# Two sums of g for the second MoE product: adding DMA transfers from GpSimd in place of VectorE, with B12, B22, T2 and T3 kept negated

## The chip, the cores and the metric

The kernel runs on one core of a Trainium2 chip. The metric is the device time of one execution in microseconds. The core has TensorE (PE in the profile, its weight loads PEld), VectorE (DVE), ScalarE (ACT), GpSimd (POOL) and SyncE (SP, which here only issues transfers). All work of an engine is done in the order in which the program gives it to that engine.

## The reference

```python
# q, k, v: (8, 12, 448, 64)
scores = scale * q @ k.T - log(S)
x = (sigmoid(scores) @ v), heads put side by side          # (3584, 768)
h = x @ w_in                                               # w_in  (768, 2048)
g = h * clip(h + 3, 0, 6) / 6
out = g @ w_out                                            # w_out (2048, 768)
```

Everything is float32.

## The kernel before

After the attention stage both MoE products are made by the scheme of Winograd and Strassen: each operand is cut into 2 x 2 blocks, sums of blocks are formed, and seven products M1 to M7 replace eight. Each float32 factor is split into two parts of a shorter type (`split`, lines 68 to 74: ScalarE casts the high part, L71, and VectorE subtracts it from the factor to get the low part, L73), and each product is three passes on TensorE.

The first product leaves h in blocks. `post` (from L404) puts each block together: ScalarE copies partial results out of PSUM (L384), VectorE adds them to the accumulator D or B (`added`, L388), ScalarE takes the relu of the block plus 3 (`relu`, L379), and VectorE makes min(relu, 6) * h (`gate`, L370). That gives the blocks B11, B21, B22 and B12 of g (without the factor 1/6). GpSimd makes T3 = B22 - B12 (L393) and T2 = T3 + B11 (L395). These six are stored to HBM (`gd`, L375).

The second product consists of 56 units (L437). A unit is one product of the seven, one of four pairs of batches, and one of two halves of the inner dimension; the order is M1, M2, M6, M7, M5, M4, M3, with 8 units for each. A unit is 3 x 4 x 3 = 36 matrix products (L657) of 128 x 128 by 128 x 448. Its operand is a block of g of 128 x 4 x 448 (896 KB). Five of the seven products take a stored block as it is. M5 (units 32 to 39) takes T1 = B12 - B11 and M4 (units 40 to 47) takes T4 = B21 - T2, which aren't stored; they are formed here:

- `g_load` (L450) loads the first block into the tile `gr` of the unit. There are three pools, one `gr` and one split tile `gx` in each, so units n and n + 3 share their tiles.
- `g_load2` (L457) loads the second block in two halves of 448 KB into two tiles of a ring of five.
- `g_sum` (L462) subtracts the halves from `gr` on VectorE.
- `g_split` splits `gr` into `gx`.

In turn n of the loop over units the program issues `g_load2` for unit n + 3, `g_load` for unit n + 4, what is planned for this turn (weight splits at each change of product, stores of results), then `g_sum` and `g_split` for unit n + 2, then the 36 products of unit n, and after each second unit `post2`: VectorE multiplies the PSUM result by 1/6 and adds it to a kept sum (`stt`, L591), once or twice. The order of the work on each engine is that of this program; no scheduler changes it. The weights of a product are loaded by SP (L472) and split at the turns around its first unit.

Of the kernel before, what the change touches and what calls it, by code (L numbers as in the profile page):

```python
# [8 lines left out]
F32 = mybir.dt.float32  # L9
# [3 lines left out]
AF = mybir.ActivationFunctionType  # L13
ALU = mybir.AluOpType
ENG = mybir.EngineType

B, H, S, D = 8, 12, 448, 64
DM, DF = 768, 2048
P = 128
# [20 lines left out]
M1, M2, M3, M4, M5, M6, M7 = range(7)  # L40
A11, A12, A21, A22, S1, S2, S3, S4 = range(8)
WEIGHT = {M1: A11, M2: A12, M3: S4, M4: A22, M5: S1, M6: S2, M7: S3}
B11, B21, B22, T4, T1, T2, T3, B12 = range(8)
MOVING = {M1: B11, M2: B21, M3: B22, M4: T4, M5: T1, M6: T2, M7: T3}
# [50 lines left out]
def tile_kernel(ctx: ExitStack, tc: tile.TileContext, qk, vP, wi, wo, outT):  # L95
    nc = tc.nc
    scale = 1.0 / math.sqrt(D)
# [4 lines left out]
    def dram_tile(name, shape):  # L102
        return dram.tile(shape, F32, name=name, tag=name)
# [4 lines left out]
    gd = {  # L108
        (p, k, h): dram_tile(f"gd_{p}_{k}_{h}", [P, FC, S])
        for p in range(NPR)  # L110
        for k in (B11, B21, B22, B12, T2, T3)
        for h in range(2)
    }
# [19 lines left out]
    bias_3 = dw.tile([P, 1], F32, name="bias_3")  # L133
# [7 lines left out]
    def ring(name, shape, dtype):  # L141
        return dw.tile(shape, dtype, tag="ring", name=name, bufs=5)

    def temp(tag, bufs, name, shape=(P, 2, S)):
        return tmp.tile(list(shape), F32, tag=tag, name=name, bufs=bufs)
# [12 lines left out]
    def at_slot(n, f, *a):  # L158
        later.setdefault(n, []).append((f, a))

    def at_unit(n, f, *a):
        plan.setdefault(n, []).append((f, a))
# [125 lines left out]
    for u in range(4 * EC):  # L288
        kh, ec = divmod(u, EC)
# [38 lines left out]
    for s in range(NS + LAG):  # L328
# [6 lines left out]
        m, r = divmod(s, LC)  # L335
# [7 lines left out]
    acc, quad = {}, {}  # L343
# [32 lines left out]

    def relu(q, k, h, tag, bufs):
        r = temp(tag, bufs, f"g{k}_{q}")
        nc.scalar.activation(r, h, AF.Relu, bias=bias_3, scale=1.0)  # L379
        return r  # L380

    def copied(q, key):
        acc[key, q] = temp("a", 4, f"{key}_{q}")
        nc.scalar.copy(acc[key, q], acc["A", q][:, :, :S])  # L384

    def added(q, key, name):
        c = temp("y", 2, f"c{name}_{q}")
        nc.vector.tensor_tensor(out=c, in0=acc[name, q][:, :, :S], in1=acc[key, q], op=ALU.add)  # L388
        return c

    def g_sums(q):
        t3 = temp("T", 3, f"gT3_{q}")
        nc.gpsimd.tensor_tensor(out=t3, in0=quad[q, B22], in1=quad[q, B12], op=ALU.subtract)  # L393
        t2 = temp("T", 3, f"gT2_{q}")
        nc.gpsimd.tensor_tensor(out=t2, in0=t3, in1=quad[q, B11], op=ALU.add)  # L395
        quad[q, T3], quad[q, T2] = t3, t2

    def c22(q, n):
        c = added(q, "u3", "D")
        at_slot(n + 1, gate, q, B22, c, relu(q, B22, c, "qk", 4))  # L400
        at_slot(n + 3, store, q, B22)

    def post(i, q, n):
        if i == M1:  # L404
            copied(q, "s1")
        elif i == M6:
            copied(q, "u2")
        elif i == M7:
            copied(q, "u3")
            if ("D", q) in acc:  # L410
                at_slot(n + 1, c22, q, n + 1)
        elif i == M5:
            if ("u3", q) in acc:
                c22(q, n)
        elif i == M2:
            c = added(q, "s1", "B")
            at_slot(n + 1, gate, q, B11, c, relu(q, B11, c, "v", 3))
            at_slot(n + 3, store, q, B11)
        elif i == M4:
            h = acc["A", q][:, :, :S]  # L420
            at_slot(n + 1, gate, q, B21, h, relu(q, B21, h, "qk", 4))
            at_slot(n + 3, store, q, B21)
        elif i == M3:
            c = added(q, "u2", "D")
            at_slot(n + 1, gate, q, B12, c, relu(q, B12, c, "qk", 4))
            at_slot(n + 2, g_sums, q)
            at_slot(n + 3, store, q, B12)
            at_slot(n + 4, store, q, T3)
            at_slot(n + 4, store, q, T2)
# [8 lines left out]
    gset, gr, gs, gx = [], {}, {}, {}  # L438
# [4 lines left out]
    PARTS = {T1: (B12, B11), T4: (B21, T2)}  # L443
# [8 lines left out]
    def g_load2(n):  # L452
        if n < len(units) and MOVING[units[n][0]] in PARTS:
            i, p, h = units[n]
            gs[n] = [ring(f"gr_{n}_{k}", [P, 2, S], F32) for k in range(2)]
            for k in range(2):
                nc.sync.dma_start(out=gs[n][k], in_=gd[p, PARTS[MOVING[i]][1], h][:, 2 * k : 2 * k + 2])  # L457

    def g_sum(n):
        for k, o in enumerate(gs.pop(n, ())):  # L460
            part = gr[n][:, 2 * k : 2 * k + 2]
            nc.vector.tensor_tensor(out=part, in0=part, in1=o, op=ALU.subtract)  # L462

    def g_split(n):
        gx[n] = gset[n % 3].tile([P, 2, FC, S], F32R, tag="gx", name=f"gx_{n}")
# [54 lines left out]
    for n, (i, q) in enumerate(seq):  # L520
        for f, a in later.pop(n, []):
            f(*a)
        w1_load(n + LA + 2)
        product(i, q, n)
        post(i, q, n)
# [31 lines left out]
    for h, n in ((0, 0), (1, 8)):  # L557
        for e in range(2 * EC):
            k, ec = divmod(e, EC)
# [9 lines left out]
    for k, i in enumerate(PHASES[1:]):  # L569
        n = 8 * (k + 1)  # L570
# [16 lines left out]
    po, so = {}, {}  # L587
    SIXTH = 1.0 / 6.0

    def stt(out, ps_in, other):  # L590
        nc.vector.scalar_tensor_tensor(out=out, in0=ps_in, scalar=SIXTH, in1=other, op0=ALU.mult, op1=ALU.add)  # L591

    def put(p, eh, k, o):
        nc.sync.dma_start(out=outT[2 * p + k, eh * EC : (eh + 1) * EC].rearrange("e p t -> p e t"), in_=o)
# [1 line left out]
    def out_tile(i, p):  # L596
        return acc_ctx[0].tile([P, EC, S], F32, tag="o", name=f"o_{i}_{p}", bufs=2)

    def kept(i, p):
        return acc_ctx[0].tile([P, EC, S], F32, tag="s", name=f"s_{i}_{p}", bufs=2 * NPR)  # L600

    def post2(i, p, n):
        t = po.pop(p)
        if n < len(units) - 1:
            t = t[:, :, :S]
        if i == M1:
            so[p] = kept(i, p)
            nc.scalar.mul(so[p], t, SIXTH)
        elif i == M6:
            stt(so[p], t, so[p])  # L610
        elif i == M7:
            so["u3", p] = kept(i, p)
            stt(so["u3", p], t, so[p])
        else:
            eh, k, other = {M2: (0, 0, p), M5: (1, 1, ("u3", p)), M4: (1, 0, ("u3", p)), M3: (0, 1, p)}[i]
            o = out_tile(i, p)
            if n == len(units) - 1:
                for ec in range(EC):
                    stt(o[:, ec], t[ec], so[other][:, ec])
                    nc.sync.dma_start(out=outT[2 * p + k, eh * EC + ec], in_=o[:, ec])  # L620
                return
            stt(o, t, so[other])
            if i == M5:
                stt(so[p], t, so[p])
            at_unit(n + 1, put, p, eh, k, o)

    for n, (i, p, h) in enumerate(units):
# [10 lines left out]
        for f, a in fetch.pop(n, []):  # L638
            f(*a)
        g_load2(n + 3)  # L640
        g_load(n + 4)
        for f, a in plan.pop(n, []):
            f(*a)
        if n + 2 < len(units):
            g_sum(n + 2)
            for _ in g_split(n + 2):
                pass
# [16 lines left out]
        if h == 1:  # L664
            post2(i, p, n)
# [34 lines left out]
```

## Time and profile before

| what | value |
|---|---|
| median of three runs | 1076.69 us (1075.88 to 1077.53) |
| the profiled execution | 1077.52 us, its span 1075.7 us |
| TensorE busy | 1067.0 us (99%) |
| VectorE busy | 743.0 us (69%) |
| ScalarE busy | 561.2 us (52%) |
| GpSimd busy | 174.2 us (16%) |
| clock granted to TensorE | 1.00 |
| second product | from about 667 us to the end |
| sums of L462 | 32 of 1084 ns, from 885.9 to 998.9 us |

Rows of groups read: line of the kernel, engine, operation, result <- operands, shapes, count | busy us, mean ns of one | idle time of the engine before them and who ended it. Rows of transfers end in the size of one and the median time in us from its issue to its landing. SPq is SP's queue of issues, L-numbers are lines of the kernel before. A share of DMA is the mean over the core's 16 DMA engines.

### The profile page before, as it was taken

How to read it: one execution, taken by the hardware profiler on the slowest of the kernel's cores; microseconds unless marked ns; L12 is line 12 of the kernel's file. 1: busy time of each engine (PE TensorE's matmuls, PEld its weight loads, DVE VectorE, ACT ScalarE, POOL GpSimd, SP SyncE). 2: the span in 40 equal slices, each digit the busy share in tenths (PEclk: the TensorE clock that was granted, in tenths of full speed). 3: DMA queues.
4: the chain of work that ended last, by engine and by line, in shares of the span. 5: the costliest groups of instructions: out<-in, count | busy, mean ns of one | idle time of the engine just before them, and what ended most of it. 6: DMA issues, size and time to landing. Idle time of an engine off the chain costs nothing.

```text
span 1075.7 us, 16712 instructions
## 1 busy us (share of the span) xinstructions
PE 1067.0 (99%) x6784; PEld 890.4 (83%) x6784; DVE 743.0 (69%) x713; ACT 561.2 (52%) x612; POOL 174.2 (16%) x82
## 2 busy tenths in 40 slices
PE   9999999999999999999999999999999999999998
PEld 4443466666999989999999999998999999999998
DVE  4679856642577987799888665987864437787642
ACT  7888988886446554664465555434332313222420
POOL 0214130000143345235322221200000000000000
PEclk9999999999999999999999999999999999999999
DMA  8887998874666877688766878869885376898741
GB/s 323 299 306 275 336 350 320 312 269 154 248 213 207 295 250 229 204 283 272 233 190 213 286 238 280 303 268 319 328 314 190 111 273 222 287 347 287 272 147 52
DMA packets 81484, 277.13 MB, mean 258 GB/s; under 512 B 7936, under 2 KB 22272, under 8 KB 81408
## 3 DMA queue, kind: packets, MB, share of 16 engines
q1 hardware_dynamic: 81408, 276.07, 73.0%
q8 instruction: 53, 0.87, 0.3%
q14 instruction: 23, 0.19, 0.0%
HBM read 189.92 MB, written 86.11 MB: 257 GB/s over the span
## 4 chain that ended last, share of the span: by engine, by line
PE 88%; DVE 4%; DMA 4%; issue 2%; ACT 2%; SPq 0%; ACTq 0%; DVEq 0%
PE po L657 32%; PE A L359 19%; PE sc L197 11%; PE pv L214 11%; PE D L359 9%; PE B L359 5%; DMA ws<-dw 2%; PE pl L657 1%; DVE w L73 1%; DMA dw<-w2S 1%; DMA qk<-qk 0%; ACT gx L71 0%; DVE x L73 0%; ACT a L199 0%; PE idle L322 0%
## 5 line engine op out<-in xcount | busy, mean ns | idle before, releaser
L657 PE MATMUL po<-gx,w 128*128 128x448 f32 x1944 | 390.0, 362 | 1.0 <-ACT w L71 0.7
L657 PEld LDWEIGHTS po<-gx,w 128*128 128x128 f32 x1944 | 364.3, 188 | 26.6 <-DVE w L73 1.4
L359 PE MATMUL A<-x,w 128*128 128x448 f32 x1152 | 236.1, 362 | 1.9 <-ACT u L384 1.9
L359 PEld LDWEIGHTS A<-x,w 128*128 128x128 f32 x1152 | 215.9, 188 | 17.6 <-ACT u L384 2.6
L71 ACT CAST gx<-gr 128x1792 fp32r<-128x1792 f32 x56 | 94.8, 1695 | 204.8 <-PE po L657 113.1
L214 PE MATMUL pv<-a,v 64*64 64x448 f32 x1344 | 198.8, 537 | 1.0 <-DVE xr L225 0.6
L197 PE MATMUL sc<-qk 64*64 64x448 f32 x1344 | 198.3, 537 | 0.4 <-ACT a L199 0.4
L199 ACT ACTIVATE a<-sc,bias_s 128x896 f32<-128x896 f32 x168 | 168.3, 1009 | 44.2 <-PE sc L197 41.3
L73 DVE TENSOR_TENSOR w<-ws,w 128x768 fp32r<-128x768 f32 x112 | 148.9, 1338 | 26.3 <-ACT w L71 26.0
L73 DVE TENSOR_TENSOR gx<-gr,gx 128x1792 fp32r<-128x1792 f32 x56 | 113.3, 2023 | 77.3 <-ACT gx L71 77.2
L214 PEld LDWEIGHTS pv<-a,v 64*64 64x64 f32 x1344 | 70.1, 133 | 62.8 <-issue 38.9
L197 PEld LDWEIGHTS sc<-qk 64*64 64x64 f32 x1344 | 69.3, 133 | 61.9 <-issue 29.2
L359 PE MATMUL D<-x,w 128*128 128x448 f32 x576 | 120.4, 362 | 0.0
L359 PEld LDWEIGHTS D<-x,w 128*128 128x128 f32 x576 | 108.1, 188 | 7.1
L71 ACT CAST w<-ws 128x768 fp32r<-128x768 f32 x112 | 93.0, 830 | 32.2 <-DMA ws<-dw 32.1
L393 POOL TENSOR_TENSOR gT<-g,g 128x896 f32<-128x896 f32 x16 | 43.5, 2721 | 269.7 <-DVE g L370 269.7
L225 DVE TENSOR_TENSOR xr<-pv,y 128x448 f32<-128x448 f32 x48 | 29.8, 621 | 53.7 <-ACT y L224 53.7
L359 PE MATMUL B<-x,w 128*128 128x448 f32 x288 | 60.2, 362 | 0.0
L379 ACT ACTIVATE g<-cD,bias 128x896 f32<-128x896 f32 x32 | 33.5, 1045 | 46.6 <-DVE cD L388 24.8
L359 PEld LDWEIGHTS B<-x,w 128*128 128x128 f32 x288 | 54.0, 188 | 3.6
L384 ACT COPY u<-A 128x896 f32<-128x896 f32 x32 | 29.0, 907 | 45.6 <-PE A L359 45.6
L388 DVE TENSOR_TENSOR cD<-D,u 128x896 f32<-128x896 f32 x32 | 34.8, 1088 | 21.0 <-ACT u L384 13.0
(65 smaller groups left out, 773.7 us busy)
## 6 DMA issues: line engine op xcount, KB each, us to landing
gr<-gd SPq DMA_DIRECT2D x56, 896.0 KB, 5.6
ws<-dw SPq DMA_DIRECT2D x112, 384.0 KB, 3.9
gd<-g SPq DMA_DIRECT2D x64, 448.0 KB, 4.6
qk<-qk SPq DMA_DIRECT2D x48, 448.0 KB, 6.7
gd<-gT SPq DMA_DIRECT2D x32, 448.0 KB, 5.2
gr<-gd SPq DMA_DIRECT2D x32, 448.0 KB, 6.1
wi<-wi SPq DMA_DIRECT2D x16, 768.0 KB, 8.0
wo<-wo SPq DMA_DIRECT2D x24, 512.0 KB, 5.2
```

The costliest lines, as they stand in the source:

```text
L71: nc.scalar.copy(hi, a)
L73: nc.vector.tensor_tensor(out=lo, in0=a, in1=hi.bitcast(F32), op=ALU.subtract)
L197: nc.tensor.matmul(out, k[halves[r], at_k], q[halves[r]], start=True, stop=True)
L199: nc.scalar.activation(a, sc[:, :, :S], AF.Sigmoid, bias=bias_s, scale=scale)
L214: nc.tensor.matmul(pv[p][halves[j], r, :S], v, a[halves[r], int(r != j) if c is None else j], start=first, stop=last)
L225: nc.vector.tensor_tensor(out=xr[b, u][:, k], in0=pv[p][:, 1, :S], in1=y, op=ALU.add)
L359: nc.tensor.matmul(t[:, j, :S], w[:, wk, j, kc], x[:, xk, kc], start=i in (M1, M2, M5) and m == 0, stop=m == 3 * KC - 1, skip_group_check= ...
L379: nc.scalar.activation(r, h, AF.Relu, bias=bias_3, scale=1.0)
L384: nc.scalar.copy(acc[key, q], acc["A", q][:, :, :S])
L388: nc.vector.tensor_tensor(out=c, in0=acc[name, q][:, :, :S], in1=acc[key, q], op=ALU.add)
L393: nc.gpsimd.tensor_tensor(out=t3, in0=quad[q, B22], in1=quad[q, B12], op=ALU.subtract)
L657: nc.tensor.matmul(po[p][ec] if n > len(units) - 3 else po[p][:, ec, :S], w[:, wk, c], x[:, xk, c], start=h == 0 and c == 0 and xk == 0 an ...
```

## The change

The blocks B12 and B22 are made negated: their h is formed as -(D + u) by a new function `less`, the relu takes a scale of -1, so it still sees h + 3, and the gate's product comes out as -g. T3 then is the negated T3, and T2 is made by subtracting B11, so it is negated too. With this the two sums become additions: -T1 = B11 + (-B12), and T4 = B21 + (-T2). `g_load2` is now one transfer of 896 KB, issued by GpSimd, that adds the second block onto `gr`; `g_sum` does nothing. Products with a negated operand (M6, M7, M5, M3) are put into the result with -1/6.

```diff
@@ -376,7 +376,7 @@
 
     def relu(q, k, h, tag, bufs):
         r = temp(tag, bufs, f"g{k}_{q}")
-        nc.scalar.activation(r, h, AF.Relu, bias=bias_3, scale=1.0)
+        nc.scalar.activation(r, h, AF.Relu, bias=bias_3, scale=-1.0 if k in (B12, B22) else 1.0)
         return r
 
     def copied(q, key):
@@ -388,15 +388,22 @@
         nc.vector.tensor_tensor(out=c, in0=acc[name, q][:, :, :S], in1=acc[key, q], op=ALU.add)
         return c
 
+    def less(q, key):
+        c = temp("y", 2, f"cD_{q}")
+        nc.vector.scalar_tensor_tensor(
+            out=c, in0=acc[key, q], scalar=-1.0, in1=acc["D", q][:, :, :S], op0=ALU.mult, op1=ALU.subtract
+        )
+        return c
+
     def g_sums(q):
         t3 = temp("T", 3, f"gT3_{q}")
         nc.gpsimd.tensor_tensor(out=t3, in0=quad[q, B22], in1=quad[q, B12], op=ALU.subtract)
         t2 = temp("T", 3, f"gT2_{q}")
-        nc.gpsimd.tensor_tensor(out=t2, in0=t3, in1=quad[q, B11], op=ALU.add)
+        nc.gpsimd.tensor_tensor(out=t2, in0=t3, in1=quad[q, B11], op=ALU.subtract)
         quad[q, T3], quad[q, T2] = t3, t2
 
     def c22(q, n):
-        c = added(q, "u3", "D")
+        c = less(q, "u3")
         at_slot(n + 1, gate, q, B22, c, relu(q, B22, c, "qk", 4))
         at_slot(n + 3, store, q, B22)
 
@@ -421,7 +428,7 @@
             at_slot(n + 1, gate, q, B21, h, relu(q, B21, h, "qk", 4))
             at_slot(n + 3, store, q, B21)
         elif i == M3:
-            c = added(q, "u2", "D")
+            c = less(q, "u2")
             at_slot(n + 1, gate, q, B12, c, relu(q, B12, c, "qk", 4))
             at_slot(n + 2, g_sums, q)
             at_slot(n + 3, store, q, B12)
@@ -452,14 +459,10 @@
     def g_load2(n):
         if n < len(units) and MOVING[units[n][0]] in PARTS:
             i, p, h = units[n]
-            gs[n] = [ring(f"gr_{n}_{k}", [P, 2, S], F32) for k in range(2)]
-            for k in range(2):
-                nc.sync.dma_start(out=gs[n][k], in_=gd[p, PARTS[MOVING[i]][1], h][:, 2 * k : 2 * k + 2])
+            nc.gpsimd.dma_start(out=gr[n], in_=gd[p, PARTS[MOVING[i]][1], h], accum_op=ALU.add)
 
     def g_sum(n):
-        for k, o in enumerate(gs.pop(n, ())):
-            part = gr[n][:, 2 * k : 2 * k + 2]
-            nc.vector.tensor_tensor(out=part, in0=part, in1=o, op=ALU.subtract)
+        pass
 
     def g_split(n):
         gx[n] = gset[n % 3].tile([P, 2, FC, S], F32R, tag="gx", name=f"gx_{n}")
@@ -587,8 +590,8 @@
     po, so = {}, {}
     SIXTH = 1.0 / 6.0
 
-    def stt(out, ps_in, other):
-        nc.vector.scalar_tensor_tensor(out=out, in0=ps_in, scalar=SIXTH, in1=other, op0=ALU.mult, op1=ALU.add)
+    def stt(out, ps_in, other, scalar=SIXTH):
+        nc.vector.scalar_tensor_tensor(out=out, in0=ps_in, scalar=scalar, in1=other, op0=ALU.mult, op1=ALU.add)
 
     def put(p, eh, k, o):
         nc.sync.dma_start(out=outT[2 * p + k, eh * EC : (eh + 1) * EC].rearrange("e p t -> p e t"), in_=o)
@@ -607,21 +610,22 @@
             so[p] = kept(i, p)
             nc.scalar.mul(so[p], t, SIXTH)
         elif i == M6:
-            stt(so[p], t, so[p])
+            stt(so[p], t, so[p], -SIXTH)
         elif i == M7:
             so["u3", p] = kept(i, p)
-            stt(so["u3", p], t, so[p])
+            stt(so["u3", p], t, so[p], -SIXTH)
         else:
             eh, k, other = {M2: (0, 0, p), M5: (1, 1, ("u3", p)), M4: (1, 0, ("u3", p)), M3: (0, 1, p)}[i]
             o = out_tile(i, p)
             if n == len(units) - 1:
                 for ec in range(EC):
-                    stt(o[:, ec], t[ec], so[other][:, ec])
+                    stt(o[:, ec], t[ec], so[other][:, ec], -SIXTH)
                     nc.sync.dma_start(out=outT[2 * p + k, eh * EC + ec], in_=o[:, ec])
                 return
-            stt(o, t, so[other])
+            sign = -SIXTH if i in (M5, M3) else SIXTH
+            stt(o, t, so[other], sign)
             if i == M5:
-                stt(so[p], t, so[p])
+                stt(so[p], t, so[p], sign)
             at_unit(n + 1, put, p, eh, k, o)
 
     for n, (i, p, h) in enumerate(units):
```

On GpSimd the transfers stand behind the last sums of the first product (L400 and L402 are L393 and L395 of before; `gT3_15` is T3 of the last of 16 groups). The last rows of before:

```order
L393 TENSOR_TENSOR gT3_14_5972<-g2_14_5830,g7_14_5940 128x896
L395 TENSOR_TENSOR gT2_14_5974<-gT3_14_5972,g0_14_5701 128x896
L393 TENSOR_TENSOR gT3_15_6104<-g2_15_6031,g7_15_6078 128x896
L395 TENSOR_TENSOR gT2_15_6106<-gT3_15_6104,g0_15_5997 128x896
L695 UNCONDITIONAL_BRANCH
L695 ISA
```

In their place now:

```order
L400 TENSOR_TENSOR gT3_14_5972<-g2_14_5830,g7_14_5940 128x896
L402 TENSOR_TENSOR gT2_14_5974<-gT3_14_5972,g0_14_5701 128x896
L400 TENSOR_TENSOR gT3_15_6104<-g2_15_6031,g7_15_6078 128x896
L402 TENSOR_TENSOR gT2_15_6106<-gT3_15_6104,g0_15_5997 128x896
L462 DMA gr_32_7504<-gd_0_0_0_87 128x1792
L462 DMA gr_33_7547<-gd_0_0_1_88 128x1792
L462 DMA gr_34_7593<-gd_1_0_0_99 128x1792
L462 DMA gr_35_7638<-gd_1_0_1_100 128x1792
L462 DMA gr_36_7691<-gd_2_0_0_111 128x1792
```

Eleven more such rows follow, up to unit 47, and then the end of the program. The number after `gr` is that of the unit.

On SP, from the load of unit 33 to that of unit 37 (`w2s` are the weights of the product M5), before:

```order
L450 DMA gr_33_7550<-gd_0_7_1_94 128x1792
L472 DMA w2s_4_0_7593<-dw2_4_0_79 128x1536
L457 DMA gr_33_0_7595<-gd_0_0_1_88 128x896
L457 DMA gr_33_1_7596<-gd_0_0_1_88 128x896
L450 DMA gr_34_7599<-gd_1_7_0_105 128x1792
L472 DMA w2s_4_1_7643<-dw2_4_1_80 128x1536
L457 DMA gr_34_0_7645<-gd_1_0_0_99 128x896
L457 DMA gr_34_1_7646<-gd_1_0_0_99 128x896
L450 DMA gr_35_7649<-gd_1_7_1_106 128x1792
L457 DMA gr_35_0_7703<-gd_1_0_1_100 128x896
L457 DMA gr_35_1_7704<-gd_1_0_1_100 128x896
L450 DMA gr_36_7707<-gd_2_7_0_117 128x1792
```

and now:

```order
L457 DMA gr_33_7547<-gd_0_7_1_94 128x1792
L475 DMA w2s_4_0_7590<-dw2_4_0_79 128x1536
L457 DMA gr_34_7593<-gd_1_7_0_105 128x1792
L475 DMA w2s_4_1_7635<-dw2_4_1_80 128x1536
L457 DMA gr_35_7638<-gd_1_7_1_106 128x1792
L457 DMA gr_36_7691<-gd_2_7_0_117 128x1792
```

The 32 loads of halves (L457 of before) are gone from this queue, and the loads of the units stand directly behind one another.

On VectorE at the change from M5 to M4 (`gx_40` is the split of unit 40, `w2_3` are the weights of M4, `o` and `s` results of unit 39), before:

```order
L73 TENSOR_TENSOR gx_40_8019<-gr_40_7913,gx_40_8019 128x1792
L73 TENSOR_TENSOR w2_3_0_0_8067<-w2s_3_0_8008,w2_3_0_0_8067 128x512
L73 TENSOR_TENSOR w2_3_0_1_8068<-w2s_3_0_8008,w2_3_0_1_8068 128x512
L73 TENSOR_TENSOR w2_3_0_2_8069<-w2s_3_0_8008,w2_3_0_2_8069 128x512
L462 TENSOR_TENSOR gr_41_7962<-gr_41_7962,gr_41_0_8010 128x896
L462 TENSOR_TENSOR gr_41_7962<-gr_41_7962,gr_41_1_8011 128x896
L73 TENSOR_TENSOR gx_41_8078<-gr_41_7962,gx_41_8078 128x1792
L591 SCALAR_TENSOR_TENSOR o_4_3_8117<-po_4_3_8022,s_6_3_7701 128x1344
L591 SCALAR_TENSOR_TENSOR s_0_3_6535<-po_4_3_8022,s_0_3_6535 128x1344
L73 TENSOR_TENSOR w2_3_1_0_8126<-w2s_3_1_8059,w2_3_1_0_8126 128x512
```

and now:

```order
L73 TENSOR_TENSOR gx_40_7971<-gr_40_7877,gx_40_7971 128x1792
L73 TENSOR_TENSOR w2_3_0_0_8016<-w2s_3_0_7965,w2_3_0_0_8016 128x512
L73 TENSOR_TENSOR w2_3_0_1_8017<-w2s_3_0_7965,w2_3_0_1_8017 128x512
L73 TENSOR_TENSOR w2_3_0_2_8018<-w2s_3_0_7965,w2_3_0_2_8018 128x512
L73 TENSOR_TENSOR gx_41_8025<-gr_41_7921,gx_41_8025 128x1792
L594 SCALAR_TENSOR_TENSOR o_4_3_8064<-po_4_3_7974,s_6_3_7688 128x1344
L594 SCALAR_TENSOR_TENSOR s_0_3_6535<-po_4_3_7974,s_0_3_6535 128x1344
L73 TENSOR_TENSOR w2_3_1_0_8070<-w2s_3_1_8011,w2_3_1_0_8070 128x512
```

The two sums are gone, and the split of unit 41 stands directly behind the weight splits.

## The prediction

> **What bounds the kernel now.** I read the page's head first, then the busy time by stage, then who waits for whom in the last 150 us, where the change lies, and last the transfers there.
>
> ```profile
> span 1075.7 us, 16712 instructions
> PE 1067.0 (99%) x6784; PEld 890.4 (83%) x6784; DVE 743.0 (69%) x713; ACT 561.2 (52%) x612; POOL 174.2 (16%) x82
> 899.00:956.00 57.00, 57.00 (x287) 53.46 (x286) 43.85 (x37) 13.89 (x11) 0.00 (x0) 1.00 0.82 299
> 956.00:1015.00 59.00, 58.65 (x294) 54.56 (x293) 42.25 (x34) 19.68 (x18) 0.00 (x0) 1.00 0.81 291
> ```
>
> The last two rows are the two stages (products M5 and M4) in which the sums stand; their columns are window, length, then busy us of PE, PEld, DVE, ACT and POOL, PE's clock, DMA share and GB/s. TensorE loses nothing in the first and 0.35 us in the second. So VectorE, though 44 of 57 us busy, isn't the bound; nothing that is taken from it can give more than TensorE waits for it. The waits from 880 to 1030 us say how much that is (columns: total us, times, longest):
>
> ```profile
> ACT gx L71 <- DVE gr L462: 69.2, 13, 9.2
> ACT gx L71 <- PE po L657: 17.6, 3, 7.2
> PEld po L657 <- DVE w L73: 0.7, 1, 0.7
> PE po L657 <- DVE w L73: 0.3, 1, 0.3
> ```
>
> The sums (L462) hold ScalarE's cast for 69.2 us in total, but only one wait reaches TensorE, 0.3 us (0.7 on its weight loads). The chain that ended last has it:
>
> ```profile
> 949.32 1.70 ACT gx L71
> 951.09 1.54 issue
> 952.99 1.89 DVE w L73 x3
> 954.88 2.02 DVE gr L462 x2
> 957.05 1.70 ACT gx L71
> 958.95 1.40 issue
> 960.72 1.55 DVE o L591
> 962.27 1.46 DVE s L591
> 964.38 93.51 PE po L657 x466
> ```
>
> The two sums of unit 41 push its cast, VectorE's results of unit 39 and the weight split of the next unit back until TensorE starts unit 41 at 964.38 instead of 0.35 us earlier. From there 466 of the 468 products of 13 units took 93.51 us: a unit is 7.2 us.
>
> **What the change removes.**
>
> ```profile
> L462 DVE TENSOR_TENSOR gr<-gr,gr 128x896 f32<-128x896 f32 x32 | 33.4, 1084 | 0.0
> gr<-gd SPq DMA_DIRECT2D x32, 448.0 KB, 6.1
> SPq L457 <- DVE gr L462: 19.7, 9, 4.6
> ```
>
> 32 sums of 1.084 us leave VectorE, 2.2 us for each of 16 units, and 32 loads of 448 KB leave SP's queue, with the 19.7 us (870 to 1010 us) that SP stood in front of them for a ring buffer; behind those waits stood the next units' loads. On the path this gives the 0.35 us above and no more: with the sums out, unit 41's cast can follow the weight casts at once and the chain is 2 us shorter than it needs to be. Gain: 0.35 us.
>
> **The edits of sign.** 32 sums in the first product turn from a two-operand form with PSUM first into a three-operand one with PSUM second; the same form stands in the trace as the gate of B21.
>
> ```profile
> L388 DVE TENSOR_TENSOR cD<-D,u 128x896 f32<-128x896 f32 x32 | 34.8, 1088 | 21.0 <-ACT u L384 13.0 <-PE D L359 7.9
> L370 DVE SCALAR_TENSOR_TENSOR g<-g,A 128x896 f32<-128x896 f32 x16 | 17.4, 1087 | 7.8 <-ACT g L379 7.6
> ```
>
> 1088 against 1087 ns: nothing. The scales of the activation (L379), of the results (L591) and POOL's add that becomes a subtraction (L395) change a constant or an operation in an instruction that stays; I take them at nothing, TensorE covering them as it covers them now. Were the 32 sums a tenth longer, that would be 32 x 0.11 = 3.5 us even with no cover at all.
>
> **What it adds.** 16 transfers of 896 KB from POOL, each of which reads g's block from HBM, reads the destination and writes it back. POOL has nothing else to do after its last sum, and only later adds queue behind a waiting add. But a link is longer: before, a unit's two operands were loaded side by side and ahead; now the add can start only when the first load has landed, and the load only when the buffer was split three units earlier. One round of a buffer, unit 37 to unit 40, as the timeline has it:
>
> ```profile
> 925.71 1.70 ACT L71 CAST gx<-gr 128x1792 fp32r<-128x1792 f32 x1 [4.23 <-DVE gr L462]
> 927.43 2.02 DVE L73 TENSOR_TENSOR gx<-gr,gx 128x1792 fp32r<-128x1792 f32 x1 [1.89 <-ACT gx L71]
> 929.49 0.32 SPq L450 DMA_DIRECT2D gr<-gd  x1
> 947.08 2.08 DVE L462 TENSOR_TENSOR gr<-gr,gr 128x896 f32<-128x896 f32 x2
> 949.32 1.70 ACT L71 CAST gx<-gr 128x1792 fp32r<-128x1792 f32 x1 [7.15 <-PE po L657]
> gr<-gd SPq DMA_DIRECT2D x19, 896.0 KB, 4.9
> ```
>
> Cast and split take 3.7 us, the load lands 4.9 us after its issue. A round may take three units, 21.6 us, so an add that lands within 21.6 - 3.7 - 4.9 = 13 us costs nothing however often it is repeated. Beyond that there is a reserve: a unit can be split as soon as the third unit before it is done, so at best 14.4 - 3.7 = 10.7 us early, and 16 adds over 3 buffers are 5.3 rounds. An add of 15 us still ends level: 5.3 x 2 = 10.7.
>
> Whether it takes less than 13 is a question of the DMA engines. From 870 to 1010 us (the GB/s row is 40 slices of 3.5 us), and the issue of unit 32's load:
>
> ```profile
> GB/s 316 203 409 297 413 177 117 406 56 350 125 207 317 289 376 171 356 289 341 189 390 412 364 414 395 209 250 357 114 252 296 320 365 293 300 378 52 379 217 371
> DMA packets 10786, 40.36 MB, mean 288 GB/s; under 512 B 1005, under 2 KB 3693, under 8 KB 10778
> q1 hardware_dynamic: 10778, 40.25, 79.2%
> gr<-gd SPq DMA_DIRECT2D x30, 448.0 KB, 6.1
> DMA to landing us min/median/max: 3.4/5.8/13.0
> 846.59 20.38 SPq L450 DMA_DIRECT2D gr<-gd  x4
> 867.02 0.90 SPq L457 DMA_DIRECT2D gr<-gd  x2
> ```
>
> (The landing row is for all transfers into gr, over the whole run; unit 32's load is the last of the four issues that end at 866.97, and its second operand's loads follow.) 40.25 MB took 79.2% of 140 us on all engines: 363 GB/s for a full share. The loads that go are 32 x 458,752 B = 14.7 MB, 40 us of the engines; the adds bring these bytes back. No row shows an adding transfer. *Lower bound:* its second read costs the engines nothing, the traffic is as before, 79%, and nothing is late: +0. *Upper bound:* twice the slowest landing of such a transfer, 26 us; a round is 3.7 + 5.8 + 26 = 35.5, and 5.3 x 13.9 - 10.7 = +63 us. Between them I take the second read as traffic like the first, since the engines' time goes with the bytes they read. Then: the adds have from 872 us (866.97 + 4.9, unit 32's load landed) to 1003.9 (unit 47 starts at 964.38 + 6 x 7.2 = 1007.6, less cast and split), 132 us. Traffic of before in that time is 0.288 x 132 = 38.0 MB, with the second read 52.7 MB. At 363 GB/s that is 145 us, 13 too long; at 414, as the best slice has it, 127 us, 5 to spare. Half of an add's reads are of SBUF, not HBM, and transfers due later can slip, so I stay below the first; waiting between load and add leaves holes, so I stay above the second: 7 us lost.
>
> The Trainium skill prices such an add: "Collectives: The Full Stack", "Part 3", says that a transfer which adds is slower by its second source read, not by the addition, and gives 62.28 against 32.35 GB/s. By that factor, 1.93, the second read would be 13.7 MB instead of 14.7 and the loss at 363 GB/s 10 us instead of 13, an estimate from that page; no run here shows it yet.
>
> Where the loss would show: a late add holds the cast, behind it in ScalarE's queue the weight casts, behind the split on VectorE the results (L591) that free PSUM, and TensorE last. The weight loads (768 KB) of the next phase make the traffic heaviest around units 39 to 42, so the stalls should begin there and not at unit 32, whose add has all the reserve.
>
> *Sum:* the profiled execution took 1077.5 us (span 1075.7), 0.8 over the median of 1076.7. -0.35 + 7 gives 1084.2 for it, 1083.4 beside the median.
>
> **Rivals.**
> 1. *Hidden.* The adds land within 13 us (15 with the reserve), since the second read is of SBUF and the engines have 21% to spare. For it: the unit's operands sit 14 us ahead, and five of the slices pass 400 GB/s. Against it: 79% plus 40 of 140 us is 108%. Time: 1076.7 - 0.35 = 1076.3. It decides as soon as the engines give over 400 GB/s, 52.7 MB / 132 us, to reads of both kinds.
> 2. *Slow adds.* An add is bound by itself and not by the engines' sum: its descriptors, made by GpSimd, or reads that wait for one another. From 15 us it costs 5.3 us for each us more; at 20 us 5.3 x 5 = 27, 1104. For it: the 13.0 us that a mere load took once, and that an add can't start before the load has landed. Against it: the median of 5.8.
> 3. *Gain beyond the 0.35 us.* SP issues earlier, VectorE is 33 us less busy. For it nothing in the waits; It would need 2 us where TensorE loses 0.35 in the two stages.
>
> **How the numbers follow.** The engines too full, +2 to +20 us, 1079 to 1096: 0.41, and the predicted time, 1083.5, is this case's. Slow adds, over +20: 0.17. Hidden: 0.38. A gain of over 0.2%: 0.04, measurement included. A difference under 0.2% (2.2 us) can't be told from none here. So faster 0.04, same 0.38, slower 0.58. The range goes from 1075.5, below the hidden case by what the three runs scatter, to 1108, an add of 21 us (5.3 x 6 = 32); above it I leave some 0.12.
>
> **What would show it.** Right: transfers of 896 KB from POOL landing in 11 to 16 us; DMA share near 95% from 880 to 1005 us; ScalarE's cast waiting for a transfer and no longer for L462; TensorE idle of some 7 us between units 39 and 48, none before; L462 gone and cD still at 1.09 us. Hidden: the same waits of the cast, landings under 13 us, TensorE without a gap at 964. Slow adds: landings of 20 us with a DMA share that does not rise, gaps from unit 34 on. The prediction is wrong in its ground if TensorE's loss lies in the first product or if landings stay at 6 us.

## The result, and the profile after

| | before | changed |
|---|---|---|
| median of 3 runs | 1076.69 us | 1085.74 us |
| lowest to highest | 1075.88 to 1077.53 us | 1083.50 to 1086.68 us |
| ratio, 95% interval | | 1.0080 (1.0062 to 1.0099) |
| profiled execution, span | 1077.5 us, 1075.7 us | 1086.7 us, 1084.9 us |

The change makes the kernel 9 us slower. The busy times of the engines after:

```profile
PE 1070.5 (99%) x6784; PEld 892.6 (82%) x6784; DVE 713.3 (66%) x681; ACT 561.4 (52%) x612; POOL 187.8 (17%) x98
```

VectorE is 29.7 us less busy and TensorE does the same number of products in a longer span. In stages (window, length, busy us of PE, PEld, DVE, ACT and POOL, PE's clock, DMA share, GB/s), the two stages with the adds, M5 and M4:

```profile
899.00:956.00 57.00, 57.00 (x287) 53.44 (x286) 26.62 (x20) 12.42 (x10) 6.08 (x8) 1.00 1.01 270
956.00:1015.00 59.00, 51.64 (x250) 46.06 (x248) 21.97 (x15) 15.69 (x13) 4.35 (x5) 0.97 0.93 261
```

M5 loses nothing at TensorE; M4 loses 7.4 us. The DMA engines are full in M5 (before: 0.82) and move fewer bytes per second than before. TensorE's pieces on the timeline (start, length, ..., idle before the piece and what ended it):

```profile
963.58 14.48 PE L661 MATMUL po<-gx,w 128*128 128x448 f32 x71 [0.65 <-DVE w L73]
978.45 14.99 PE L661 MATMUL po<-gx,w 128*128 128x448 f32 x72 [0.40 <-DVE gx L73]
995.03 14.48 PE L661 MATMUL po<-gx,w 128*128 128x448 f32 x71 [1.59 <-DVE gx L73]
1012.87 0.74 PE L661 MATMUL po<-gx,w 128*128 128x448 f32 x1 [3.37 <-ACT gx L71]
```

The pieces begin with units 41, 43, 45 and 47 of M4 (a unit is 7.2 us), and the gaps reach 3.37 us. The chain that ended last leads through units 41, 44 and 47, which share a buffer (start, length, what; rows left out are marked):

```profile
956.24 1.70 ACT gx L71
...
960.02 8.04 DMA gr<-gd
...
968.71 12.75 DMA gr<-gd
...
981.55 1.70 ACT gx L71
...
985.33 13.05 DMA gr<-gd
...
999.03 12.01 DMA gr<-gd
...
1011.13 1.69 ACT gx L71
...
1014.93 52.06 PE po L661 x251
1066.99 14.41 PE pl L661 x72
```

Here one buffer is followed through two rounds: cast and split of unit 41, load and add of unit 44, cast and split of unit 44 (981.55), load and add of unit 47, cast of unit 47 (1011.13). The rounds last 25.3 and 29.6 us, where three units last 21.6. The three rounds before them in this buffer were too long as well: its casts start at 883.08 (unit 32), 907.66, 929.74 and 956.24 us (unit 41), 24.6, 22.1 and 26.5 us apart. All five together are 20 us over five times 21.6. Unit 32 was split some 11 us ahead of its turn; that reserve was used up on the way, and the 9 us that are left are the delay with which unit 47 sets in.

From the start of unit 41 to that of the last two units (`pl`) it was 93.51 us before and is 1066.99 - 963.58 = 103.41 us now: 9.9 us more. Unit 41 itself starts 0.8 us earlier than before, so the difference at the end is 9.1 us, and the spans differ by 9.2. The 9.9 us are the delays before units 43, 45 and 47, 0.47, 2.18 and 5.50 us (each start against 14.4 us per two units), and 1.66 us in the seven units from 47 to 53: 52.06 us where 7 x 7.2 = 50.4 were due, one product having gone ahead. These last 1.66 us aren't waits. Windows of 4 us, with the columns of the stages above:

```profile
1012.00:1016.00 4.00, 1.81 (x4) 1.27 (x5) 3.15 (x2) 4.00 (x6) 0.00 (x0) 0.50 0.11 20
1016.00:1020.00 4.00, 4.00 (x16) 3.62 (x15) 4.00 (x5) 1.56 (x1) 0.00 (x0) 0.70 0.93 343
```

After the gap before unit 47 the granted clock is 0.50 and then 0.70; TensorE is busy all of 1016 to 1020 us and does 16 products, where a unit's 36 in 7.2 us are 20 in 4. The Trainium skill, "TensorE: Matmul & The Clock Gate", Part 1, says that the array falls to half its clock after an idle window of about 3.4 us and needs about 3.4 us of work to come back. For the way back the trace agrees: 1.66 us lost at half clock are 3.3 us of work. For the way down it doesn't: the clock falls at about 1011.6 us (1.00 from 1011.0 to 1011.5 us, 0.57 from 1011.5 to 1012.0), 2.1 us after TensorE stopped at 1009.5.

The transfers from 870 to 1010 us (queue: packets, MB, share of the 16 engines; then issues with their count, size and median us to landing):

```profile
q0 software_dynamic: 2303, 14.68, 54.0%
q1 hardware_dynamic: 5523, 23.45, 44.7%
gr<-gd SPq DMA_DIRECT2D x17, 896.0 KB, 8.8
gr<-gd POOLq DMA_DIRECT2D x16, 896.0 KB, 10.7
```

The sixteen adds alone hold the engines for 54.0% of 140 = 75.6 us; with everything else the engines are full. An add lands after 10.7 us, a load after 8.8 (before: 4.9). And who waits from 880 to 1040 us (total us, times, longest):

```profile
ACT gx L71 <- DMA gr<-gd: 80.3, 13, 12.5
```

ScalarE's cast, which waited for VectorE's sums before, waits for the add.

The sign edits:

```profile
L393 DVE SCALAR_TENSOR_TENSOR cD<-u,D 128x896 f32<-128x896 f32 x32 | 34.7, 1084 | 19.0 <-ACT u L384 11.0 <-PE D L359 8.0
```

1084 ns where the old form took 1088.

### The profile page after: what moved, and what is told of

Read it like the earlier page. It is cut to its first block, busy times and chain, and to the rows that moved or that the text cites. A ratio compares the mean times of both kernels' runs of the same rounds, so it can differ in the third digit from the quotient of the medians.

```text
span 1084.9 us, 16668 instructions
## 1 busy us (share of the span) xinstructions
PE 1070.5 (99%) x6784; PEld 892.6 (82%) x6784; DVE 713.3 (66%) x681; ACT 561.4 (52%) x612; POOL 187.8 (17%) x98
## 4 chain that ended last, share of the span: by engine, by line
PE 85%; DMA 7%; DVE 4%; ACT 2%; issue 1%; SPq 0%; ACTq 0%; POOLq 0%; DVEq 0%
PE po L661 27%; PE A L359 20%; PE sc L197 11%; PE pv L214 11%; PE D L359 10%; DMA gr<-gd 5%; PE B L359 5%; PE pl L661 1%; DMA ws<-dw 1%; DVE gx L73 1%; DMA dw<-w2S 1%; ACT gx L71 1%; DVE w L73 1%; ACT a L199 0%; DVE x L73 0%
## 5 line engine op out<-in xcount | busy, mean ns | idle before, releaser
L73 DVE TENSOR_TENSOR w<-ws,w 128x768 fp32r<-128x768 f32 x112 | 151.2, 1358 | 25.6 <-ACT w L71 25.3
L400 POOL TENSOR_TENSOR gT<-g,g 128x896 f32<-128x896 f32 x16 | 43.5, 2719 | 268.4 <-DVE g L370 251.9
L462 POOL DMA_DIRECT2D gr<-gd x16 | 14.1, 878 | 307.0 <-DVE s L594 194.8
## 6 DMA issues: line engine op xcount, KB each, us to landing
gr<-gd POOLq DMA_DIRECT2D x16, 896.0 KB, 10.7
```

Source lines behind the costliest of these rows:

```text
L73: nc.vector.tensor_tensor(out=lo, in0=a, in1=hi.bitcast(F32), op=ALU.subtract)
L462: nc.gpsimd.dma_start(out=gr[n], in_=gd[p, PARTS[MOVING[i]][1], h], accum_op=ALU.add)
```

## The experiments

Two theories stand against each other. The prediction's (the engines): the second read of the adds makes more work than the DMA engines have time for. The rival (the round): the time goes with the round of a buffer, split, load and add one after the other; it is longer than three units leave it, and full engines matter only through the durations in it. Each ratio below is against the kernel before, run on the same chip beside it. In the first four expectations the rival still was a chain that takes its time whatever it reads; the round as it is told here was set up after those runs.

### e_plain: the add turned into a load

Undoes the adding alone: the transfer from GpSimd overwrites the buffer. The sums of M5 and M4 are left out.

```diff
-            nc.gpsimd.dma_start(out=gr[n], in_=gd[p, PARTS[MOVING[i]][1], h], accum_op=ALU.add)
+            nc.gpsimd.dma_start(out=gr[n], in_=gd[p, PARTS[MOVING[i]][1], h])
```

> The changed kernel, but GpSimd's 16 transfers copy the second block over the first and don't add it, so the sums of M5 and M4 are left out. Same queue, same wait for the first load, same bytes written, one read less. Theory 1 (the adds' second read fills the DMA engines): DMA share of 870 to 1010 us falls from 99% to about 80%, the transfers from GpSimd land in 5 to 7 us and not 10.7, TensorE has no gap after unit 32, 1076.3 us. Rival (the chain: load, then a transfer made by GpSimd, in series, whatever it reads): gaps at units 41 to 47 as before them, 1082 to 1086 us.

1075.32 us, ratio 0.9994 (0.9985 to 1.0004). TensorE in M4, and the transfers from 870 to 1010 us:

```profile
956.00:1015.00 59.00, 59.00 (x296) 55.31 (x296) 28.82 (x22) 17.54 (x15) 2.12 (x4) 1.00 0.78 278
```

```profile
q0 software_dynamic: 2304, 14.68, 28.9%
gr<-gd SPq DMA_DIRECT2D x20, 896.0 KB, 6.2
gr<-gd POOLq DMA_DIRECT2D x16, 896.0 KB, 6.3
```

The place of the transfer, its queue and its wait for the load cost nothing; the loss is in the adding. The same bytes hold the engines 40.5 us here and 75.6 us when they are added: an add is 1.87 times a load, and the second read is 35.1 us. The 0.35 us gap at unit 41 is gone, as the prediction had it. A chain that costs its time whatever it reads is ruled out, since there are no gaps. Both theories told above fit: the engines aren't full, and a round is 3.7 + 6.2 + 6.3 = 16.2 us.

### e_signs: the signs alone

```diff
-            nc.gpsimd.dma_start(out=gr[n], in_=gd[p, PARTS[MOVING[i]][1], h], accum_op=ALU.add)
+            gs[n] = [ring(f"gr_{n}_{k}", [P, 2, S], F32) for k in range(2)]
+            for k in range(2):
+                nc.sync.dma_start(out=gs[n][k], in_=gd[p, PARTS[MOVING[i]][1], h][:, 2 * k : 2 * k + 2])
...
+            nc.vector.tensor_tensor(out=part, in0=part, in1=o, op=ALU.add)
```

> Only the edits of sign; the sums stay on VectorE as additions, the halves on SP's queue. Theory 1: no difference to the kernel before, 1076.7 us, the sums formed by the new three-operand form still 1.09 us each. Rival (the edits of sign carry a part of their own, since the changed kernel reached the second product 1.4 us earlier): 1075.3 us.

1076.01 us, ratio 0.9998 (0.9989 to 1.0007). The edits of sign cost nothing that can be measured.

### e_dummy: the engines filled without adds

The kernel before, with 16 more loads of 768 KB from GpSimd, for which nobody waits; a small sum on GpSimd ahead of each paces them.

```diff
+            more = extra.tile([P, 1536], F32, tag="more", name=f"more_{n}")
+            few = gr[n][:, 0, :64]
+            nc.gpsimd.tensor_tensor(out=more[:, :64], in0=few, in1=few, op=ALU.add)
+            nc.gpsimd.dma_start(out=more, in_=gd[p, PARTS[MOVING[i]][1], h].rearrange("p c s -> p (c s)")[:, :1536])
...
+    extra = ctx.enter_context(tc.tile_pool(name="extra", bufs=2, reuse_waits="tile"))
```

> The kernel before with 16 more loads of 768 KB (12.6 MB) into unused tiles, issued by GpSimd each when the first block of a unit of M5 or M4 has landed (a small copy on GpSimd sets that time). Nothing waits for them. They take as much of the DMA engines (12.6 MB / 363 GB/s = 35 us) as the adds took above plain loads (54.0% of 140 us = 76 us against 40). Theory 1: share near 95 to 100%, loads land later, gaps of TensorE in M4, 1081 to 1087 us. Rival (chain): the sums' operands still come side by side, 1076.7 us.

1076.33 us, ratio 1.0000 (0.9991 to 1.0009). The stage M4, and the transfers from 870 to 1010 us:

```profile
956.00:1015.00 59.00, 58.34 (x291) 54.15 (x291) 43.49 (x34) 20.74 (x19) 6.43 (x10) 1.00 1.01 397
```

```profile
DMA packets 12919, 52.52 MB, mean 375 GB/s; under 512 B 1232, under 2 KB 3920, under 8 KB 12911
gr<-gd SPq DMA_DIRECT2D x19, 896.0 KB, 7.6
gr<-gd SPq DMA_DIRECT2D x30, 448.0 KB, 10.0
```

The engines are as full as with the adds, the loads that somebody waits for land 2.7 and 3.9 us later than before, and nothing is lost. Theory 1 gave 1081 to 1087 us. The extra loads may land when they like, but all of their 12.58 MB moved within these 140 us. Here the loads that are waited for are side by side and ahead of their use. Full engines alone, then, are not the cause, and the theory of the engines falls in this form. The run also gives a size that the prediction lacked: 52.52 MB in 140 us, 375 GB/s, is what full engines moved, of loads and stores.

### e_noputs: less traffic

The change without the stores of M5's and M4's results, which are left out.

```diff
-            at_unit(n + 1, put, p, eh, k, o)
+            if i not in (M5, M4):
+                at_unit(n + 1, put, p, eh, k, o)
```

> The changed kernel without the stores of the results of M5 and M4 (8 stores, 5.5 MB, 15 us of the engines at 363 GB/s; these parts of the output are left out). Theory 1: the 13 us of excess are covered, the loss falls to 0 to 2 us, 1076.5 to 1079 us, adds land in 9 to 10 us. Rival (chain): the adds wait for their loads as before, 1083 to 1086 us.

1078.65 us (1074.48 to 1082.82), ratio 1.0023 (1.0007 to 1.0039): 6.6 of the 9 us come back.

```profile
gr<-gd SPq DMA_DIRECT2D x19, 896.0 KB, 7.6
gr<-gd POOLq DMA_DIRECT2D x16, 896.0 KB, 10.6
```

The adds land as late as with the stores, 10.6 us, the loads 1.2 us earlier: a round is 3.7 + 7.6 + 10.6 = 21.9 us, 0.3 over the 21.6. That a small part of the traffic decides so much fits both theories. By its expectation theory 1 had the time right and the landings wrong (9 to 10 us), and the chain's 1083 to 1086 us missed. What is left of the loss in the profiled execution (1078.38 us) is one gap, before unit 41, whose cast waited until 956.36 us for its add:

```profile
963.69 94.97 PE L662 MATMUL po<-gx,w 128*128 128x448 f32 x466 [2.37 <-DVE w L73]
```

The granted clock behind this gap of 2.37 us is 0.50 from 963.69 to 965 us and 1.00 again from 967 us; the 466 products take 94.97 us where they took 93.51 before.

### e_halves: the load and the add in halves

```diff
-            nc.sync.dma_start(out=gr[n], in_=gd[p, first, h])
+            for k in range(2 if MOVING[i] in PARTS else 1):
+                part = slice(2 * k, 2 * k + 2) if MOVING[i] in PARTS else slice(0, FC)
+                nc.sync.dma_start(out=gr[n][:, part], in_=gd[p, first, h][:, part])
...
-            nc.gpsimd.dma_start(out=gr[n], in_=gd[p, PARTS[MOVING[i]][1], h], accum_op=ALU.add)
+            for k in range(2):
+                part = slice(2 * k, 2 * k + 2)
+                nc.gpsimd.dma_start(out=gr[n][:, part], in_=gd[p, PARTS[MOVING[i]][1], h][:, part], accum_op=ALU.add)
```

> The changed kernel with load and add of a unit cut in halves of 448 KB: the first half's add can run while the second half is still loaded. Bytes and the engines' time are the same, the chain from load to split is shorter by about half a load (4 us). Theory 1 (the engines' time alone sets the loss): as the changed kernel, 1083 to 1087 us. Theory 2 (full engines make load and add slow, 8.8 and 10.7 us, and only since the one follows the other does a round, 3.7 + 8.8 + 10.7 = 23.2 us, exceed three units, 21.6): a round of about 19 us, the loss falls to 0 to 3 us, 1076 to 1079 us.

1078.72 us, ratio 1.0024 (1.0014 to 1.0034).

```profile
q0 software_dynamic: 4608, 14.68, 54.7%
q1 hardware_dynamic: 7746, 23.79, 46.9%
```

The work of the engines is the same and they are as full (101.6%), but the add of a first half needs only the first half's load, and 6.5 us of the 9 come back. Work that doesn't fit would have been lost as before: theory 1 gave 1083 to 1087 us.

### e_4buf: a fourth buffer

Units 32 to 47 take turns in four buffers, so a round may last four units, 28.8 us. The adds and the bytes are the same.

```diff
...
-            gr[n] = gset[n % 3].tile([P, FC, S], F32, tag="gr", name=f"gr_{n}")
+            at = (n + 2) % 4 if 32 <= n < 48 else (n + 2) % 3 if n >= 48 else n % 3
+            gr[n] = [*gset, more][at].tile([P, FC, S], F32, tag="gr", name=f"gr_{n}")
...
-        g_load2(n + 3)
-        g_load(n + 4)
+        for m in (n + 4, n + 5):
+            if n == (m - 5 if 33 <= m <= 48 else m - 4):
+                g_load(m)
+                g_load2(m)
```

> The changed kernel with four buffers in place of three for the blocks of units 32 to 47, so load and add of a unit start one unit (7.2 us) earlier; bytes and the adds are the same. Theory 2: a round may take 28.9 us, so 23.2 fits and nothing is late, 1075.5 to 1077 us. Theory 1: the engines stay full, 139 us of work for 131 us; the earlier start gives 7 of the 8 missing once, 1077 to 1080 us. In both the adds stay at 10 us or more.

1075.86 us, ratio 0.9993 (0.9984 to 1.0003): the whole loss is gone.

```profile
q0 software_dynamic: 2304, 14.68, 51.9%
q1 hardware_dynamic: 6286, 26.17, 48.5%
gr<-gd SPq DMA_DIRECT2D x19, 896.0 KB, 10.9
gr<-gd POOLq DMA_DIRECT2D x16, 896.0 KB, 11.5
```

```profile
956.00:1015.00 59.00, 58.52 (x291) 54.18 (x290) 27.59 (x20) 19.87 (x18) 3.48 (x4) 1.00 0.97 300
```

The engines are full, loads and adds land even later than in the change, and TensorE loses 0.48 us in M4. A round is 3.7 + 10.9 + 11.5 = 26.1 us and may be 28.8. By their expectations the theories lie close here (1077 to 1080 and 1075.5 to 1077 us), since the earlier start also gives the engines 7 us more. What tells them apart is what moved: 40.96 MB from 870 to 1010 us, the sixteen adds among them, against 38.24 MB in the changed kernel. So the engines can do the work in time, and what was too long was the chain through three buffers. It equals the kernel before and doesn't beat it.

### e_2buf: one buffer fewer

The opposite: two buffers for units 32 to 47, a round may last 14.4 us.

```diff
-            gr[n] = gset[n % 3].tile([P, FC, S], F32, tag="gr", name=f"gr_{n}")
+            at = n % 2 if 32 <= n < 48 else (n + 2) % 3 if n >= 48 else n % 3
+            gr[n] = gset[at].tile([P, FC, S], F32, tag="gr", name=f"gr_{n}")
...
-        g_load2(n + 3)
-        g_load(n + 4)
+        for m in (n + 3, n + 4):
+            if n == (m - 3 if 34 <= m <= 47 else m - 4):
+                g_load(m)
+                g_load2(m)
```

> The changed kernel with two buffers in place of three for the blocks of units 32 to 47: the same bytes and the same adds, but a round of split, load and add has two units, 14.4 us, not three. Theory 2 (the round decides): with the landings eased to 5.5 and 8 us a round of 17.5 us, 3 us too long in 8 rounds less the reserve of 10.7, +14 us; with today's landings +60; so 1090 to 1135 us, while the share of the DMA engines falls under 90%. Theory 1 (full engines alone): the same work for the engines, 1083 to 1087 us, share near 100%.

1121.78 us, ratio 1.0426 (1.0408 to 1.0443).

```profile
956.00:1015.00 59.00, 45.54 (x197) 39.08 (x197) 23.10 (x17) 13.25 (x12) 5.22 (x6) 0.91 0.86 236
```

```profile
gr<-gd SPq DMA_DIRECT2D x14, 896.0 KB, 8.1
gr<-gd POOLq DMA_DIRECT2D x13, 896.0 KB, 8.1
```

The window is M4's in the other runs; here it holds the end of M5 and the first half of M4. The engines have 14% to spare in it (15% in M4 itself, from 971 to 1047 us), and the loss is five times as large. By the medians a round is 3.7 + 8.1 + 8.1 = 19.9 us, 5.5 over; eight rounds make 44 us, and 45 were measured. That leaves out two things that nearly cancel. In the trace the buffer of the odd units goes through eight rounds from its cast at 874.91 us (unit 31) to that at 1044.17 us (unit 47), 21.2 us each and 54 us over in all, and unit 31 was split some 11 us ahead of its turn, which leaves 43 us. The round sets the time here with engines that aren't full.

### e_m5 and e_m5_look: the adds in M5 alone

The sums of M4 stay on VectorE, as before.

```diff
+            if i == M5:
+                nc.gpsimd.dma_start(out=gr[n], in_=gd[p, PARTS[MOVING[i]][1], h], accum_op=ALU.add)
+                return
+            gs[n] = [ring(f"gr_{n}_{k}", [P, 2, S], F32) for k in range(2)]
...
+            nc.vector.tensor_tensor(out=part, in0=part, in1=o, op=ALU.add)
```

> Half of the change: adds by transfer only for the eight units of M5, VectorE adds for M4. The 8 adds put 17 us of excess on the engines while the reserve lasts. Theory 1: 8 x 2.3 = 18 us more for M5's 58 us, engines full in M5 and back under 85% in M4, 0 to 2 us lost, 1076 to 1078.5 us. Theory 2: 2.7 rounds x 1.6 us = 4 us, inside the reserve of 10.7, no loss: 1076 to 1077 us.

1081.23 us (1076.38 to 1084.95), ratio 1.0047 (1.0031 to 1.0062). That is more than either theory gave. The execution with a profile was the shortest of the ten and showed a gap of 0.95 us at unit 41, so the same kernel was looked at again:

> The kernel of half the change once more, for a trace of one of its usual executions: the one profiled was the fastest of ten (1076.4 us, median 1081.2). If the loss is the round's, as theory 2 has it, TensorE's gaps lie at units 40 to 43, where the last adds of M5 and the weight loads of M4 meet and VectorE's sums set in again; if it lies elsewhere, in the first product say, theory 2 does not explain this kernel.

1079.06 us. TensorE's timeline, and the chain that ended last:

```profile
965.86 54.31 PE L668 MATMUL po<-gx,w 128*128 128x448 f32 x270 [3.06 <-DVE w L73]
```

```profile
905.96 1.70 ACT gx L71
...
916.13 13.89 DMA gr<-gd
...
930.13 1.70 ACT gx L71
...
934.87 10.72 DMA gr<-gd
...
948.63 2.01 DVE gr L472 x2
...
950.79 1.70 ACT gx L71
```

The loss is one gap, at unit 41, where the last buffers filled by adds meet VectorE's sums again. A round in M5 took 930.13 - 905.96 = 24.2 us. By the chain, the load behind it landed late, its sums came late on VectorE, and so did the casts of unit 40 (950.79) and unit 41 (958.52). The split of unit 39, whose cast waited for its add until 941.94, ended on VectorE just as that load landed (945.7 us), so the two can't be told apart. The kernel before was already 0.35 us late at this very unit (its chain in the prediction), so nothing of the reserve was left there to take it up. That is read from one execution. Why the median loses 5 us and this one 3 is told in part by the mean granted clock of the ten: 1.000 in the three of 1079.3 to 1080.0 us, 0.998 in the four of 1081.1 to 1081.7, 0.997 in the two of 1084.1 and 1085.0 (0.999 in the shortest), and 0.002 of 1080 us are 2.2 us. This execution kept a clock of 1.00 behind its gap of 3.06 us, where e_noputs lost it in one of 2.37; what decides that no run here shows.

### e_stored: the sums made earlier, and stored

On the kernel before: T1 and T4 are made by GpSimd in the first product and stored, so that the second product has neither sums nor adds.

```diff
...
+        t4 = temp("T", 3, f"gT4_{q}")
+        nc.gpsimd.tensor_tensor(out=t4, in0=quad[q, B21], in1=t2, op=ALU.subtract)
+        t1 = quad[q, B12]
+        nc.gpsimd.tensor_tensor(out=t1, in0=t1, in1=quad[q, B11], op=ALU.subtract)
...
-            at_slot(n + 3, store, q, B12)
+            at_slot(n + 6, store, q, T4)
+            at_slot(n + 6, store, q, T1)
...
-    PARTS = {T1: (B12, B11), T4: (B21, T2)}
+    PARTS = {}
```

> No sums in the second product at all: GpSimd forms T1 = B12 - B11 and T4 = B21 - T2 beside T2 and T3 in the first product, T1 is stored in place of B12, T4 in addition, M5 and M4 load them as they are. The engines lose 14.7 MB of loads in the second product and gain 7.3 MB of stores in the first. Theory: TensorE's 0.35 us are all there is to win in the second product, and GpSimd's 90 us more fit in the first: 1075.5 to 1077 us. Rival: GpSimd's two-operand sums hold up VectorE's gates and stores of SP in the first product: 1078 to 1085 us.

1102.31 us, ratio 1.0242 (1.0226 to 1.0257), above both the forecast and its rival. The first product from 260 to 667 us, and the costliest group of VectorE, which is its weight split:

```profile
260.00:667.00 407.00, 393.40 (x1945) 365.42 (x1940) 342.77 (x241) 213.10 (x243) 200.29 (x68) 0.98 0.75 246
```

```profile
L73 DVE TENSOR_TENSOR w<-ws,w 128x768 fp32r<-128x768 f32 x112 | 168.1, 1507 | 25.6 <-ACT w L71 25.3
```

TensorE is idle 13.6 us in this window alone, where it was idle 2.1 before; GpSimd is busy 200 us instead of 129, and VectorE's split, untouched by the edit, takes 1507 ns instead of 1338. In the second product TensorE is busy all the time in M5 and M4, which lie some 25 us later here: 57.00 of 57 us from 924 to 981 and 59.00 of 59 to 1040. So the sums gone from there are worth what the prediction said, next to nothing, and the price of making them elsewhere is all that counts. The edit also stores one block more per group and keeps two blocks longer; what each of this costs was not separated.

### e_alone: the transfers by themselves

Only transfers of 896 KB, and the few operations that give them a source and an order; all else is left out. `two` are loads from GpSimd, one at a time; `three` are adds one at a time; `four` are adds and `five` loads in three buffers, three in flight.

> Transfers of 896 KB from HBM by themselves, all other work of the kernel left out: 6 loads from SP, 6 from GpSimd and 6 adds from GpSimd, each waiting for the one before it; then 9 adds and 9 loads from GpSimd into three tiles, three in flight. If an add costs its second read in full: alone about 2.2 us more than a load of about 4 us (917,504 B / 420 GB/s), and three in flight 4.4 us each against 2.2. If GpSimd's descriptors set its price, its plain loads too are several us above SP's. If its reads wait for one another, an add in the middle of three takes over 6 us.

```profile
two<-src POOLq DMA_DIRECT2D x6, 896.0 KB, 4.8
three<-src POOLq DMA_DIRECT2D x6, 896.0 KB, 7.3
```

An add lands 2.5 us after a load from the same queue would. With three in flight, first and last issue of the steady part:

```profile
145.77 0.87 POOL L76 DMA_DIRECT2D four<-src  x1 [5.28 <-DMA four<-src]
167.25 0.86 POOL L76 DMA_DIRECT2D four<-src  x1 [3.44 <-DMA four<-src]
195.96 0.53 POOL L81 DMA_DIRECT2D five<-src  x1 [3.48 <-DMA five<-src]
207.71 0.53 POOL L81 DMA_DIRECT2D five<-src  x1 [2.15 <-DMA five<-src]
```

Five steps each: an add every 4.30 us (213 GB/s of result), a load every 2.35 us (390 GB/s), a factor of 1.83. The issue takes GpSimd 0.87 us for an add and 0.53 for a load; neither is near the 4.30. With three in flight the adds keep the engines full (a share of 1.02 from 140 to 170 us, at 209 GB/s), as the loads do (0.99 from 193 to 210 us, at 399 GB/s). So neither GpSimd's making of an add nor the add by itself sets the pace, and a cost of nearly two reads fits it.

## Why the prediction was right, and where it was not

The direction, the size (1083.5 forecast, 1085.74 measured) and the place were right, the size in part by luck. By its steps:

- **The gain, 0.35 us.** Right for the sums alone: e_plain has no gap at unit 41, and its time is the same as before within the measurement. In the changed kernel the gain didn't come: the gap before unit 41 is 0.65 us, ended by a weight split whose cast had waited 3.65 us for its load. Nothing more was to be had, as M5 and M4 of e_stored show.
- **The signs, 0.** Right: 1084 against 1088 ns, and e_signs at 0.9998.
- **An add reads twice.** Right in kind: 35.1 us of engines where 40 were taken. The factor is 1.87 in the kernel and 1.83 alone, not 2. The Trainium skill's factor, 1.93 ("Collectives: The Full Stack", Part 3; told there of a ring of ranks), is nearer than 2 and still above both.
- **The landing.** The row said 11 to 16 us as a mark of being right; the median is 10.7, and the two adds in the chain took 12.0 and 12.8. The add stayed inside the 13 us that the budget gave it. By the prediction's own marks that alone would have meant "hidden".
- **The budget of a round, 21.6 - 3.7 - 4.9 = 13 us.** This is the step that failed, in one of its terms: 4.9 us was the load's landing before the change. With the adds in the same engines the load takes 8.8 us, and in the last round 13.05. The budget for an add was 9.1 us, not 13. By medians a round is 3.7 + 8.8 + 10.7 = 23.2 us, 1.6 over, and 5.3 rounds of that, 8.5 us, would still fit into the reserve of 10.7. The rounds of the trace are longer than the sum of the medians, 25.6 us in the mean over the five of one buffer (22.1 to 29.6), so some 3 us of the reserve were left before the last two.
- **"145 us of work in 132", taken at 7 us.** The sum came out near for the wrong reason, and by luck: 7 was chosen between 13 too long and 5 to spare, and no run shows a loss by work that doesn't fit. Engines as full as these lost nothing in e_dummy, nor with all of the adds in e_4buf; engines that had 14% to spare lost 45 us in e_2buf. The second read is the origin of the loss, since e_plain has none, but it acts by lengthening load and add, which stand in series, and not by work that doesn't fit.
- **Where it shows.** Right: nothing before unit 39, gaps of 0.65, 0.40, 1.59, 3.37 and (after one product of unit 47) 1.32 us from unit 41 to 47, 7.3 us in all against "some 7". The share of the DMA engines, forecast near 95%, was 99% from 870 to 1010 us. What was missed is 1.66 us at a reduced clock after the last gap; no term of the sum had it.
- **The rivals.** "Hidden" falls by the result, but e_4buf is that rival with one buffer more: the same adds, 0.9993. "Slow adds" falls: three adds in flight take 4.30 us each. "A gain" had nothing to gain from.

Still open: the size of the loss in e_m5 beyond its clock, and what made the load of unit 47 take 13.05 us, since several transfers shared the engines with it and none was taken away alone.

## What to carry to other kernels

An adding transfer cost the engines almost twice a load here (1.87 and 1.83), and it can't start until its destination has landed; so price the round split, load, add against the number of buffers, with landings as they will be when the extra read is in the engines. One buffer more brought back here the whole loss, though the busy engines (51.9% and 48.5% of the 140 us) seemed to forbid it. And before work is moved from an engine that is off the path, look what the path can gain by it: here it was 0.35 us.

## What the hardware showed that was not expected

- DMA engines at a share of 1.01 through a stage cost nothing as long as the transfers had slack (e_dummy, 375 GB/s over 140 us).
- In the changed kernel TensorE's granted clock halved 2.1 us into a gap of 3.37 us and cost 1.66 us more than the wait (0.50 and 0.70 in the windows from 1012 to 1020 us). A gap of 2.37 us halved it too (e_noputs); one of 3.06 us did not (e_m5_look).
- More sums on GpSimd lengthened VectorE's splits: with GpSimd busy 200 instead of 129 us of 407, the split went from 1338 to 1507 ns, and the kernel lost 2.4% (e_stored). That the one causes the other was not separated by a run.
